# An attention block on one core: p transposed as pairs of bf16, the engines' orders rearranged, and V loaded in two pieces

## The chip, the cores and the metric

The kernel runs on one core of a Trainium2 chip. Its time is the device time of one execution in microseconds (us); "before" is the median of three runs. One further execution was recorded by the profiler, and all durations below come from that one.

## What is computed

The reference projects x to queries for 32 heads of width 192, attends over a cache of 512 keys and values, and projects the result back:

```python
B, Sq, D = 8, 112, 640
H, Sk, Dh = 32, 512, 192
q = (x @ wq).reshape(B, Sq, H, Dh).transpose(0, 2, 1, 3)
scores = einsum("bhqd,bhkd->bhqk", q, k_cache) * Dh ** -0.5
p = softmax(scores, axis=-1)
o = einsum("bhqk,bhkd->bhqd", p, v_cache)
out = o.transpose(0, 2, 1, 3).reshape(B, Sq, H * Dh) @ wo
```

All inputs and the output are bf16. The two caches are 50 MB each and are read once.

## The kernel before

The work is cut into 64 groups. A group is four heads of one batch element (two pairs of heads, `pr` 0 and 1). `groups` lists them by head group (eight heads) and batch element. Every operation is entered into a `Plan` as one block on one engine, with the tokens that it reads and writes; the order in which blocks are entered is the order in which an engine runs them, and `Plan.solve` turns tokens into semaphore waits. A token with fewer slots than versions makes a writer wait for the readers of the version that it overwrites.

A loop over `g` (lines 540 to 606) enters one iteration of a software pipeline. In an iteration TensorE (PE) works on four groups at once:

- scores of group g: `s_mains` (L302, L304, contraction 128) for heads 2, 3, 0, 1, then `s_tails` (L317, L319, contraction 64, two at a time in the two halves of the array), into PSUM banks 0 to 3;
- `pv_tails` of g-2 (L404), the last 64 columns of p times V, two heads side by side;
- `pt` of g-1 (L367), the transposes of the normalised p, four blocks of 112x128 for each head, into bank PTB; pair 0 before the output projection and pair 1 between the two `q_stage` blocks;
- `o_stage` of g-2 (L432 and, for the last 128 output columns, L446), the output projection;
- `q_stage` of g+2 (L261), the queries, into banks 0 and 1;
- `pv_mains` of g-1 (L389).

VectorE (DVE) takes the scores out of PSUM with the row minimum of the negated scores (`smax`, L331), copies transposed p (`evac_pt`, L377), inverts the row sums (L350), normalises p (`norm`, L357) and, at the end of its iteration, adds the output projection to an accumulator (`oacc`, L468/L469). ScalarE (ACT) copies the results of PV (`evac_m` L413, `evac_t` L419), computes the four exponentials (L341) and copies the queries (`evac_q`, L271) after the second and after the fourth exponential. GpSimd (POOL) makes a copy of the queries with the partition halves swapped (L282, L284). For the last head group, `o_final` (L480) transposes the sums back and `evac_final` (L488) copies them out.

All loads are issued by one queue, SP's, in a fixed order: for two groups at a time K, K, V, V (L220, L229) and then at most one piece of wq or wo (L237, L245) for the next head group; these pieces end with group 51. K is loaded by a transposing DMA, 768 KB for a group; V by one plain DMA of 128 rows, each with four runs of 1,536 bytes. There are six buffers for K and six for V. The key order inside a row of 512 scores is that of K's transposed layout; `QJ` says which quarter of V belongs to which quarter of p.

Of the kernel before, what the change touches and what calls it, by code (L numbers as in the profile page):

```python
# [142 lines left out]
def build_mha_kernel(nc, x, k_cache, v_cache, wq, wo, out):  # L143
# [12 lines left out]
    QJ = [0, 2, 1, 3]  # L156
# [18 lines left out]
    with ExitStack() as es:  # L175
# [17 lines left out]
        ident = sb("ident", [128, 128], BF16)  # L193
        nmx = sb("nmx", [SQ, 8], F32)
# [4 lines left out]
        psb = ps[:].bitcast(BF16)  # L199

# [23 lines left out]
        def load_v(g):  # L224
            u, hg, b, half = group(g)
            h0 = hg * HG + 4 * half

            def fn(e):
                return e.dma_start(vt[g % NVB][:, :, :], v_cache[b, h0:h0 + 4].rearrange("u (r q) d -> r u (q d)", q=4))  # L229
            P.add("SP", f"v{g}", fn, writes=[("vt", g)], dma=True)  # L230
# [63 lines left out]
        def s_mains(g, h):  # L294
            em, _, om, _ = q_tiles(g, h)
            pr, cols = h // 2, slice(256 * (h % 2), 256 * (h % 2) + 256)
            n = 2 * g + pr
            k = kt[g % NKB]
            cs = slice(h * 128, (h + 1) * 128)

            def fn(e):
                e.matmul(ps[0:SQ, 2 * pr, cols], em, k[:, :, 0, cs], start=(h % 2 == 0), stop=False,  # L302
                         skip_group_check=True)
                return e.matmul(ps[0:SQ, 2 * pr + 1, cols], om, k[:, :, 2, cs], start=(h % 2 == 0), stop=False,  # L304
                                skip_group_check=True)
            P.add("PE", f"S{g}.{h}", fn, reads=[("kt", g), ("qs", n), ("w", n)],
                  writes=[(f"bank{2 * pr + i}", 2 * g) for i in range(2)])

        def s_tails(g, pr):
            k = kt[g % NKB]  # L310

            def fn(e):
                for h in (2 * pr, 2 * pr + 1):
                    _, lo, _, hi = q_tiles(g, h)
                    cols = slice(256 * (h % 2), 256 * (h % 2) + 256)
                    cs = slice(h * 128, (h + 1) * 128)
                    e.matmul(ps[0:SQ, 2 * pr, cols], lo, k[0:64, :, 1, cs], start=False, stop=True,  # L317
                             skip_group_check=True)
                    mm = e.matmul(ps[0:SQ, 2 * pr + 1, cols], hi, k[64:128, :, 1, cs], start=False, stop=True,  # L319
                                  skip_group_check=True)  # L320
                return mm
            n = 2 * g + pr
            P.add("PE", f"St{g}.{pr}", fn, reads=[("kt", g), ("qs", n), ("w", n)],
                  writes=[(f"bank{2 * pr + i}", 2 * g) for i in range(2)])

        def smax(g, h):
            n = 4 * g + h
            pr, cols = h // 2, slice(256 * (h % 2), 256 * (h % 2) + 256)

            def fn(e):  # L330
                return e.tensor_scalar(s_sb[:, n % 4, :].rearrange("p (a c) -> p a c", a=2),  # L331
                                       ps[0:SQ, 2 * pr:2 * pr + 2, cols], -scale, None, op0=ALU.mult, op1=ALU.min,
                                       accum_out=nmx[:, n % 8:n % 8 + 1])
            P.add("DVE", f"mx{g}.{h}", fn, reads=[(f"bank{2 * pr + i}", 2 * g) for i in range(2)],
                  writes=[("s", n), ("nmx", n)])
# [17 lines left out]
        def norm(g, h):  # L353
            n = 4 * g + h

            def fn(e):
                return e.tensor_scalar(pn_sb[:, n % 8, :], p_sb[:, n % 4, :], rinv[:, n % 8:n % 8 + 1], None,  # L357
                                       op0=ALU.mult)
            P.add("DVE", f"nm{g}.{h}", fn, reads=[("p", n), ("rinv", n // 2)], writes=[("pn", n)])

        def pt(g, pr):
            def fn(e):
                for h in range(2):
                    n = 4 * g + 2 * pr + h
                    for j in range(4):
                        c = (4 * h + j) * SQ
                        mm = e.transpose(psb[:, PTB, c:c + SQ], pn_sb[:, n % 8, j * 128:(j + 1) * 128],  # L367
                                         ident[0:SQ, 0:SQ])
                return mm
            P.add("PE", f"PT{g}.{pr}", fn, reads=[("pn", 4 * g + 2 * pr), ("pn", 4 * g + 2 * pr + 1), ("ident", 0)],  # L370
                  writes=[("ptb", 2 * g + pr)])

        def evac_pt(g, pr):
# [4 lines left out]
            P.add("DVE", f"ep{g}.{pr}", fn, reads=[("ptb", n)], writes=[("pT", n)])  # L378

        def pv_mains(g, pr):  # L380
# [3 lines left out]
            def fn(e):  # L384
                for h in range(2):
                    u = 2 * pr + h
                    for j in range(4):
                        d0 = QJ[j] * 192 + 64 * h
                        mm = e.matmul(ps[:, MB, (2 * pr + h) * SQ:(2 * pr + h + 1) * SQ], v[:, u, d0:d0 + 128],  # L389
                                      pT[:, n % 3, (4 * h + j) * SQ:(4 * h + j + 1) * SQ],  # L390
                                      start=(j == 0), stop=(j == 3))
# [3 lines left out]
        def pv_tails(g):  # L395
            v = vt[g % NVB]

            def fn(e):
                for pr in range(2):
                    n = 2 * g + pr  # L400
                    for j in range(4):
                        for h in range(2):
                            d0 = QJ[j] * 192 + (128 if h == 0 else 0)
                            mm = e.matmul(ps[64 * h:64 * h + 64, TB, pr * SQ:(pr + 1) * SQ],  # L404
                                          v[:, 2 * pr + h, d0:d0 + 64],
                                          pT[:, n % 3, (4 * h + j) * SQ:(4 * h + j + 1) * SQ],
                                          start=(j == 0), stop=(j == 3))
# [15 lines left out]
        def o_stage(g):  # L423
# [13 lines left out]
            P.add("PE", f"O{g}", fn, reads=[("oT", g)] + wos, writes=[("ob", 2 * u)])  # L437
# [17 lines left out]
        def oacc(g):  # L455
# [15 lines left out]
            for part, name, tok in ((1, "acc5", ("tb", 2 * g + 1)), (0, "acc4", ("ob", 2 * u))):  # L471
# [3 lines left out]
        def o_final(g):  # L475
            u, hg, b = groups[g][:3]

            def fn(e):
                for c in range(DC):
                    mm = e.transpose(psb[0:SQ, OB, c * 128:(c + 1) * 128], oTf[:, b % 2, c, :], ident[:, :])  # L480
                return mm
            P.add("PE", f"OF{b}", fn, reads=[("oTf", b), ("ident", 0)], writes=[("ob", 2 * u + 1)])

        def evac_final(g):
            u, hg, b = groups[g][:3]

            def fn(e):
                return e.activation(o_out[b], psb[0:SQ, OB, 0:D], ACTF.Copy)  # L488
            P.add("ACT", f"ef{b}", fn, reads=[("ob", 2 * u + 1)], writes=[("oo", b)])
# [6 lines left out]
        def init_pool():  # L496
# [4 lines left out]
                  reads=[("id0", 0)], writes=[("ident", 0)])  # L501

# [37 lines left out]
        for g in range(-2, NG + 3):  # L540
            qver = 2 * g + 1

            if ok(g):
                for h in (2, 3, 0, 1):
                    s_mains(g, h)
                s_tails(g, 0)
                s_tails(g, 1)
            fin = ok(g - 3) and groups[g - 3][1] == NHG - 1 and groups[g - 3][5]
            if fin:
                o_final(g - 3)  # L550
            if ok(g - 2):
                pv_tails(g - 2)
# [10 lines left out]
            if ok(g - 1):  # L563
                pv_mains(g - 1, 0)
                pv_mains(g - 1, 1)

            if ok(g - 2):
                evac_m(g - 2)
            if fin:
                evac_final(g - 3)  # L570
            if ok(g - 2):
                evac_t(g - 2)
            if ok(g):
                exp(g, 0)
                exp(g, 1)
            if ok(g + 2):
                evac_q(g + 2, 0, qver)
            if ok(g):
                exp(g, 2)
                exp(g, 3)  # L580
            if ok(g + 2):
                evac_q(g + 2, 1, qver)

# [5 lines left out]
            if ok(g):  # L589
                smax(g, 2)  # L590
                smax(g, 3)
            if ok(g - 1):
# [8 lines left out]
            if ok(g - 2) and groups[g - 2][5]:  # L601
                oacc(g - 2)
# [80 lines left out]
```

## Time and profile before

| | |
|---|---|
| median of three runs | 501.61 us (496.06 to 502.46) |
| profiled execution: device time | 505.89 us |
| profiled execution: span, first to last instruction | 503.9 us |
| mean granted TensorE clock | 0.986 |
| busy: PE / DVE / ACT / POOL | 452.3 / 361.7 / 288.1 / 86.5 us |
| moved by DMA | 119.88 MB, mean 238 GB/s |
| V loads, K loads | 64 each; median from issue to landing 6.6 and 8.5 us |

A line of a group view reads: line, engine, operation, output from input, count, then busy time and mean duration of one. A PE duration holds the pipeline's depth too, so the pace of a row of matmuls is read from the start times in the timeline, not from the duration of one. "PEld" is the loading of the stationary operand. "SPq" in a chain or a timeline is the SP queue while it issues a DMA: an issue lasts longer when the descriptors find no room.

### The profile page before, as it was taken

Reading aid. Unit: us, or ns where it says so; the run is one execution under the profiler, and the core shown is the slowest. Engines: PE = TensorE matmul, PEld = TensorE weight load, DVE = VectorE, ACT = ScalarE, POOL = GpSimd, SP = SyncE. Lnnn points to the kernel's source line nnn. Section 1 sums busy time; section 2 is a strip of 40 time slices with the busy share of each in tenths; the row PEclk is TensorE's granted clock in tenths of the full one; section 3 lists DMA queues with packets and bytes.
Section 4 is the critical chain, followed back from the end, with each engine's and each line's share of the span. In section 5 each row is a group of like instructions: output and inputs, shape, how many; then the busy total and the mean of one; then the engine's idle time right before and its main releaser. Section 6 shows DMA issues by size and latency. Waiting matters only on the chain.

```text
span 503.9 us, 18575 instructions
## 1 busy us (share of the span) xinstructions
PE 452.3 (90%) x7976; PEld 403.8 (80%) x7976; DVE 361.7 (72%) x1105; ACT 288.1 (57%) x778; POOL 86.5 (17%) x262
## 2 busy tenths in 40 slices
PE   4749898989998988998997999999999899999985
PEld 4639787878987977887987888898888788888974
DVE  0728867787888777767776788787777777787781
ACT  2616645556656545655654566565566567666762
POOL 1202212112112212212211112211121121112100
PEclk9989989999999999999999999999999999999999
DMA  8999999999999999999999999999999999999910
GB/s 188 227 267 263 255 301 273 221 223 256 258 278 249 236 228 230 238 260 265 231 200 252 270 264 245 276 264 231 233 262 246 272 228 258 245 257 230 269 44 23
DMA packets 255026, 119.88 MB, mean 238 GB/s; under 512 B 204896, under 2 KB 254944, under 8 KB 254944
## 3 DMA queue, kind: packets, MB, share of 16 engines
q1 hardware_dynamic: 254944, 118.70, 106.3%
q8 instruction: 62, 1.02, 0.9%
q14 instruction: 20, 0.16, 0.1%
HBM read 66.06 MB, written 1.15 MB: 133 GB/s over the span
## 4 chain that ended last, share of the span: by engine, by line
DMA 35%; PE 30%; SPq 25%; ACT 4%; DVE 3%; issue 2%; POOL 0%; DVEq 0%
DMA kt<-in_k_cache_dram 32%; SPq L220 20%; PE ps L432 6%; PE ps L261 5%; PE ps L367 3%; PE ps L302 3%; ACT p_sb L341 3%; PE ps L404 2%; PE ps L304 2%; PE ps L317 2%; SPq L229 2%; PE ps L389 2%; DMA wo_sb<-in_wo_dram 2%; PE ps L446 1%; SPq L245 1%
## 5 line engine op out<-in xcount | busy, mean ns | idle before, releaser
L331 DVE TENSOR_SCALAR_CACHE_REDUCE s_sb<-ps 112x512 f32<-112x512 f32 x256 | 165.5, 683 | 50.2 <-PE ps L319 50.2
L341 ACT ACTIVATE p_sb<-s_sb,nmx 112x512 bf16<-112x512 f32 x256 | 181.2, 712 | 3.7 <-DVE s_sb L331 3.7
L261 PE MATMUL ps<-xT,wq_sb 128*128 128x112 bf16 x1920 | 118.6, 216 | 16.0 <-DMA wq_sb<-in_wq_dram 7.3
L377 DVE COPY pT<-ps 128x896 bf16<-128x896 bf16 x128 | 79.8, 623 | 69.9 <-PE ps L367 69.9
L261 PEld LDWEIGHTS ps<-xT,wq_sb 128*128 128x128 bf16 x1920 | 104.0, 100 | 16.6 <-DMA wq_sb<-in_wq_dram 7.3
L282 POOL COPY wt<-qs 64x168 int32<-64x168 int32 x128 | 44.4, 347 | 383.9 <-ACT qs L271 383.9
L271 ACT ACTIVATE qs<-ps 128x336 bf16<-128x336 f32 x128 | 56.6, 442 | 84.7 <-PE ps L261 84.6
L432 PE MATMUL ps<-oT,wo_sb 128*128 128x112 bf16 x1536 | 86.6, 213 | 3.4 <-DMA wo_sb<-in_wo_dram 1.9
L357 DVE TENSOR_SCALAR pn_sb<-p_sb,rinv 112x512 bf16<-112x512 bf16 x256 | 83.3, 368 | 4.5
L432 PEld LDWEIGHTS ps<-oT,wo_sb 128*128 128x128 bf16 x1536 | 76.6, 98 | 10.8 <-ACT p_sb L341 3.1
L419 ACT ACTIVATE oT<-ps 128x224 bf16<-128x224 f32 x64 | 22.8, 356 | 105.9 <-PE ps L404 105.9
L367 PE MATMUL ps<-ident,pn_sb 112*128 112x112 bf16 x1024 | 72.7, 214 | 0.0
L389 PE MATMUL ps<-pT,vt 128*128 128x112 bf16 x1024 | 61.5, 213 | 1.0 <-DVE pT L377 1.0
L302 PE MATMUL ps<-kt,qs 128*112 128x256 bf16 x128 | 38.0, 297 | 25.1 <-DMA kt<-in_k_cache_dram 20.1
L367 PEld LDWEIGHTS ps<-ident,pn_sb 112*128 112x128 bf16 x1024 | 55.2, 98 | 5.2 <-issue 0.2
L389 PEld LDWEIGHTS ps<-pT,vt 128*128 128x128 bf16 x1024 | 53.7, 98 | 1.5 <-DVE pT L377 1.4
L341 ACT ACTIVATION_READ_ACCUMULATOR p_sb<-s_sb,nmx 112x1 f32 x256 | 48.8, 190 | 0.0
L302 PEld LDWEIGHTS ps<-kt,qs 128*112 128x112 bf16 x128 | 16.5, 129 | 35.2 <-DMA kt<-in_k_cache_dram 13.3
L284 POOL COPY wt<-qs 64x168 int32<-64x168 int32 x128 | 41.4, 323 | 7.9
L404 PE MATMUL ps<-pT,vt 128*64 128x112 bf16 x1024 | 37.9, 217 | 0.0
L404 PEld LDWEIGHTS ps<-pT,vt 128*64 128x64 bf16 x1024 | 28.3, 111 | 10.9 <-issue 10.1
L413 ACT ACTIVATE oT<-ps 128x448 bf16<-128x448 f32 x64 | 34.4, 537 | 4.6 <-PE ps L389 4.6
(33 smaller groups left out, 489.3 us busy)
## 6 DMA issues: line engine op xcount, KB each, us to landing
vt<-in_v_cache_dram SPq DMA_DIRECT2D x64, 768.0 KB, 6.6
wq_sb<-in_wq_dram SPq DMA_DIRECT2D x16, 480.0 KB, 9.0
wo_sb<-in_wo_dram SPq DMA_DIRECT2D x16, 480.0 KB, 8.4
out_dram<-accT SPq DMA_DIRECT2D x8, 140.0 KB, 7.1
kt<-in_k_cache_dram SPq DMA_TRANSPOSE x64, 8.5
xT<-in_x_dram SPq DMA_TRANSPOSE x3, 4.3
```

The lines of the kernel that those rows point to most:

```text
L220: return e.dma_start_transpose(kt[g % NKB][:].rearrange("p a m c -> p (a m) c"), k_cache[b, h0:h0 + 4].rearrange("u (r q) d -> (u r) (q d) ...
L261: mm = e.matmul(ps[:, pr, c * SQ:(c + 1) * SQ], wq_sb[:, hg % 2, dc, c0 + 128 * c:c0 + 128 * (c + 1)], xT[:, dc, b * SQ:(b + 1) * SQ], sta ...
L271: return e.activation(qs[:, n % 6, :, :], ps[:, pr, 0:3 * SQ].rearrange("p (c s) -> p c s", c=3), ACTF.Copy)
L302: e.matmul(ps[0:SQ, 2 * pr, cols], em, k[:, :, 0, cs], start=(h % 2 == 0), stop=False, skip_group_check=True)
L331: return e.tensor_scalar(s_sb[:, n % 4, :].rearrange("p (a c) -> p a c", a=2), ps[0:SQ, 2 * pr:2 * pr + 2, cols], -scale, None, op0=ALU.mu ...
L341: return e.activation(p_sb[:, n % 4, :], s_sb[:, n % 4, :], ACTF.Exp, bias=nmx[:, n % 8:n % 8 + 1], scale=-1.0, accum_out=rsum[:, n % 8:n ...
L357: return e.tensor_scalar(pn_sb[:, n % 8, :], p_sb[:, n % 4, :], rinv[:, n % 8:n % 8 + 1], None, op0=ALU.mult)
L367: mm = e.transpose(psb[:, PTB, c:c + SQ], pn_sb[:, n % 8, j * 128:(j + 1) * 128], ident[0:SQ, 0:SQ])
L377: return e.tensor_copy(pT[:, n % 3, :], psb[:, PTB, 0:8 * SQ])
L389: mm = e.matmul(ps[:, MB, (2 * pr + h) * SQ:(2 * pr + h + 1) * SQ], v[:, u, d0:d0 + 128], pT[:, n % 3, (4 * h + j) * SQ:(4 * h + j + 1) * SQ],
L404: mm = e.matmul(ps[64 * h:64 * h + 64, TB, pr * SQ:(pr + 1) * SQ], v[:, 2 * pr + h, d0:d0 + 64], pT[:, n % 3, (4 * h + j) * SQ:(4 * h + j ...
L432: mm = e.matmul(ps[:, OB, dcc * SQ:(dcc + 1) * SQ], wo_sb[:, wb, 3 * (2 * half + pr) + c, dcc * 128:(dcc + 1) * 128], oT[:, g % 3, pr, c, ...
```

## The change

It has four parts. V of a group is loaded by two DMAs, rows 0 to 119 and rows 120 to 127, on the same semaphore. p is transposed as words: `smax` writes the scores of two key quarters interleaved, so that two neighbouring bf16 of the normalised p form one 4-byte word; `pt` transposes the 512 bf16 of a head as 256 words in two blocks of 112x128 f32 against an f32 identity, and PV reads its moving operand with a step of two elements (`p_block`); `norm` raises p to at least 2^-126, so that no word is subnormal. The order on PE becomes: tails of the scores before their mains, `pv_tails` of g-1 at the end of the iteration, after `pv_mains`, and `o_final` just before it. On ACT the four exponentials come in a row and both `evac_q` after them; on DVE `oacc` comes before the second `evac_pt`.

```diff
@@ -153,7 +153,7 @@
     scale = float(DH) ** -0.5
-    QJ = [0, 2, 1, 3]
+    TINY = 2.0 ** -126
     NKB, NVB = 6, 6
@@ -191,6 +191,7 @@
         ident = sb("ident", [128, 128], BF16)
+        identf = sb("identf", [SQ, SQ], F32)
         nmx = sb("nmx", [SQ, 8], F32)
@@ -198,6 +199,9 @@
         psb = ps[:].bitcast(BF16)
+        pnw = pn_sb[:].rearrange("p n k -> p (n k)").bitcast(F32)
         o_out = [accT[0:SQ, b, :, :].rearrange("p c s -> p (c s)").bitcast(BF16)[:, 0:D] for b in range(B)]
@@ -225,9 +229,12 @@
             h0 = hg * HG + 4 * half
-            def fn(e):
-                return e.dma_start(vt[g % NVB][:, :, :], v_cache[b, h0:h0 + 4].rearrange("u (r q) d -> r u (q d)", q=4))
-            P.add("SP", f"v{g}", fn, writes=[("vt", g)], dma=True)
+            def fn(r0, r1):
+                src = v_cache[b, h0:h0 + 4].rearrange("u (r q) d -> r u (q d)", q=4)
+                return lambda e: e.dma_start(vt[g % NVB][r0:r1, :, :], src[r0:r1])
+            for r0, r1 in ((0, 120), (120, 128)):
+                P.add("SP", f"v{g}.{r0}", fn(r0, r1), writes=[("vt", g)], dma=True)
         def load_wq(hg, lp, after=()):
@@ -299,9 +306,9 @@
             def fn(e):
-                e.matmul(ps[0:SQ, 2 * pr, cols], em, k[:, :, 0, cs], start=(h % 2 == 0), stop=False,
+                e.matmul(ps[0:SQ, 2 * pr, cols], em, k[:, :, 0, cs], start=False, stop=True,
                          skip_group_check=True)
-                return e.matmul(ps[0:SQ, 2 * pr + 1, cols], om, k[:, :, 2, cs], start=(h % 2 == 0), stop=False,
+                return e.matmul(ps[0:SQ, 2 * pr + 1, cols], om, k[:, :, 2, cs], start=False, stop=True,
                                 skip_group_check=True)
@@ -314,9 +321,9 @@
                     cs = slice(h * 128, (h + 1) * 128)
-                    e.matmul(ps[0:SQ, 2 * pr, cols], lo, k[0:64, :, 1, cs], start=False, stop=True,
+                    e.matmul(ps[0:SQ, 2 * pr, cols], lo, k[0:64, :, 1, cs], start=(h % 2 == 0), stop=False,
                              skip_group_check=True)
-                    mm = e.matmul(ps[0:SQ, 2 * pr + 1, cols], hi, k[64:128, :, 1, cs], start=False, stop=True,
+                    mm = e.matmul(ps[0:SQ, 2 * pr + 1, cols], hi, k[64:128, :, 1, cs], start=(h % 2 == 0), stop=False,
                                   skip_group_check=True)
@@ -328,7 +335,7 @@
             def fn(e):
-                return e.tensor_scalar(s_sb[:, n % 4, :].rearrange("p (a c) -> p a c", a=2),
+                return e.tensor_scalar(s_sb[:, n % 4, :].rearrange("p (c a) -> p a c", a=2),
                                        ps[0:SQ, 2 * pr:2 * pr + 2, cols], -scale, None, op0=ALU.mult, op1=ALU.min,
@@ -354,28 +361,32 @@
             def fn(e):
-                return e.tensor_scalar(pn_sb[:, n % 8, :], p_sb[:, n % 4, :], rinv[:, n % 8:n % 8 + 1], None,
-                                       op0=ALU.mult)
+                return e.tensor_scalar(pn_sb[:, n % 8, :], p_sb[:, n % 4, :], rinv[:, n % 8:n % 8 + 1], TINY,
+                                       op0=ALU.mult, op1=ALU.max)
             P.add("DVE", f"nm{g}.{h}", fn, reads=[("p", n), ("rinv", n // 2)], writes=[("pn", n)])
...
                     n = 4 * g + 2 * pr + h
-                    for j in range(4):
-                        c = (4 * h + j) * SQ
-                        mm = e.transpose(psb[:, PTB, c:c + SQ], pn_sb[:, n % 8, j * 128:(j + 1) * 128],
-                                         ident[0:SQ, 0:SQ])
-                return mm
-            P.add("PE", f"PT{g}.{pr}", fn, reads=[("pn", 4 * g + 2 * pr), ("pn", 4 * g + 2 * pr + 1), ("ident", 0)],
-                  writes=[("ptb", 2 * g + pr)])
+                    for t in range(2):
+                        c = (2 * h + t) * SQ
+                        w0 = (n % 8) * (SK // 2) + t * 128
+                        mm = e.transpose(ps[:, PTB, c:c + SQ], pnw[:, w0:w0 + 128], identf[:, :])
+                return mm
+            P.add("PE", f"PT{g}.{pr}", fn, reads=[("pn", 4 * g + 2 * pr), ("pn", 4 * g + 2 * pr + 1), ("identf", 0)],
+                  writes=[("ptb", 4 * g + pr)])
         def evac_pt(g, pr):
...
                 return e.tensor_copy(pT[:, n % 3, :], psb[:, PTB, 0:8 * SQ])
-            P.add("DVE", f"ep{g}.{pr}", fn, reads=[("ptb", n)], writes=[("pT", n)])
+            P.add("DVE", f"ep{g}.{pr}", fn, reads=[("ptb", 4 * g + pr)], writes=[("pT", n)])
+        def p_block(n, h, q):
+            return pT[:, n % 3, :].rearrange("p (h t s a) -> p h t a s", h=2, t=2, a=2)[:, h, q // 2, q % 2, :]
         def pv_mains(g, pr):
@@ -385,10 +396,9 @@
                     for j in range(4):
-                        d0 = QJ[j] * 192 + 64 * h
+                        d0 = j * 192 + 64 * h
                         mm = e.matmul(ps[:, MB, (2 * pr + h) * SQ:(2 * pr + h + 1) * SQ], v[:, u, d0:d0 + 128],
-                                      pT[:, n % 3, (4 * h + j) * SQ:(4 * h + j + 1) * SQ],
-                                      start=(j == 0), stop=(j == 3))
+                                      p_block(n, h, j), start=(j == 0), stop=(j == 3))
                 return mm
@@ -400,11 +410,10 @@
                         for h in range(2):
-                            d0 = QJ[j] * 192 + (128 if h == 0 else 0)
+                            d0 = j * 192 + (128 if h == 0 else 0)
                             mm = e.matmul(ps[64 * h:64 * h + 64, TB, pr * SQ:(pr + 1) * SQ],
                                           v[:, 2 * pr + h, d0:d0 + 64],
-                                          pT[:, n % 3, (4 * h + j) * SQ:(4 * h + j + 1) * SQ],
-                                          start=(j == 0), stop=(j == 3))
+                                          p_block(n, h, j), start=(j == 0), stop=(j == 3))
                 return mm
@@ -434,7 +443,7 @@
                 return mm
-            P.add("PE", f"O{g}", fn, reads=[("oT", g)] + wos, writes=[("ob", 2 * u)])
+            P.add("PE", f"O{g}", fn, reads=[("oT", g)] + wos, writes=[("ob", u)])
             if not last:
@@ -468,7 +477,7 @@
                 return go
-            for part, name, tok in ((1, "acc5", ("tb", 2 * g + 1)), (0, "acc4", ("ob", 2 * u))):
+            for part, name, tok in ((1, "acc5", ("tb", 2 * g + 1)), (0, "acc4", ("ob", u))):
                 P.add("DVE", f"oa{part}.{u}", fn(part), reads=[tok] + ([] if copy else [(name, ver - B)]),
@@ -477,16 +486,17 @@
                 for c in range(DC):
-                    mm = e.transpose(psb[0:SQ, OB, c * 128:(c + 1) * 128], oTf[:, b % 2, c, :], ident[:, :])
-                return mm
-            P.add("PE", f"OF{b}", fn, reads=[("oTf", b), ("ident", 0)], writes=[("ob", 2 * u + 1)])
+                    mm = e.transpose(psb[0:SQ, PTB, c * 128:(c + 1) * 128], oTf[:, b % 2, c, :], ident[:, :])
+                return mm
+            P.add("PE", f"OF{b}", fn, reads=[("oTf", b), ("ident", 0)],
+                  writes=[("ptb", 4 * (g + 1) + 2)])
         def evac_final(g):
...
             def fn(e):
-                return e.activation(o_out[b], psb[0:SQ, OB, 0:D], ACTF.Copy)
-            P.add("ACT", f"ef{b}", fn, reads=[("ob", 2 * u + 1)], writes=[("oo", b)])
+                return e.activation(o_out[b], psb[0:SQ, PTB, 0:D], ACTF.Copy)
+            P.add("ACT", f"ef{b}", fn, reads=[("ptb", 4 * (g + 1) + 2)], writes=[("oo", b)])
         def store(b):
@@ -499,6 +509,8 @@
                   reads=[("id0", 0)], writes=[("ident", 0)])
+            P.add("POOL", "id2", lambda e: e.tensor_copy(identf[:], ident[0:SQ, 0:SQ]), reads=[("ident", 0)],
+                  writes=[("identf", 0)])
         GH = B * GPU
@@ -541,15 +553,11 @@
             if ok(g):
-                for h in (2, 3, 0, 1):
+                s_tails(g, 1)
+                s_tails(g, 0)
+                for h in range(4):
                     s_mains(g, h)
-                s_tails(g, 0)
-                s_tails(g, 1)
-            fin = ok(g - 3) and groups[g - 3][1] == NHG - 1 and groups[g - 3][5]
-            if fin:
-                o_final(g - 3)
-            if ok(g - 2):
-                pv_tails(g - 2)
+            fin = ok(g - 2) and groups[g - 2][1] == NHG - 1 and groups[g - 2][5]
             if ok(g - 1):
@@ -563,23 +571,22 @@
                 pv_mains(g - 1, 1)
+            if fin:
+                o_final(g - 2)
+            if ok(g - 1):
+                pv_tails(g - 1)
             if ok(g - 2):
                 evac_m(g - 2)
-            if fin:
-                evac_final(g - 3)
-            if ok(g - 2):
                 evac_t(g - 2)
             if ok(g):
-                exp(g, 0)
-                exp(g, 1)
+                for h in range(4):
+                    exp(g, h)
             if ok(g + 2):
                 evac_q(g + 2, 0, qver)
-            if ok(g):
-                exp(g, 2)
-                exp(g, 3)
-            if ok(g + 2):
                 evac_q(g + 2, 1, qver)
+            if fin:
+                evac_final(g - 2)
             if ok(g):
@@ -589,6 +596,8 @@
                 smax(g, 3)
+            if ok(g - 2) and groups[g - 2][5]:
+                oacc(g - 2)
             if ok(g - 1):
@@ -598,8 +607,6 @@
                 norm(g, 3)
-            if ok(g - 2) and groups[g - 2][5]:
-                oacc(g - 2)
             if ok(g + 2):
```

## The prediction

> **What bounds the kernel now.** I read the page first, then the windows, the SP queue's timeline, PE's timeline and last the DMA packet records.
>
> ```profile
> PE 452.3 (90%) x7976; PEld 403.8 (80%) x7976; DVE 361.7 (72%) x1105; ACT 288.1 (57%) x778; POOL 86.5 (17%) x262
> DMA  8999999999999999999999999999999999999910
> ...
> q1 hardware_dynamic: 254944, 118.70, 106.3%
> q8 instruction: 62, 1.02, 0.9%
> ```
>
> Two resources look full: PE at 90%, the DMA engines at 9 tenths or more nearly everywhere. An average does not say which sets the pace, so I cut the span.
>
> ```profile
> 200.00:300.00 100.00, 92.57 (x1644) 82.43 (x1643) 73.52 (x225) 57.54 (x158) 17.43 (x52) 0.98 1.14 247
> 402.00:474.00 72.00, 71.49 (x1275) 63.40 (x1272) 55.00 (x169) 46.20 (x124) 13.41 (x40) 1.00 1.13 242
> ```
>
> From 402 us, when wq and wo are all loaded, PE is busy for 71.49 of 72 us: PE sets the pace there. In the chain its output projections of every second group start at 401.55 and 473.30, five pairs of groups apart: 14.35 us a pair. From 200 to 300 PE idles 7%, and SP's queue shows why.
>
> ```profile
> 261.56 1.08 SPq L229 DMA_DIRECT2D vt<-in_v_cache_dram  x2
> 262.69 0.50 SPq L245 DMA_DIRECT2D wo_sb<-in_wo_dram  x1
> 263.24 12.91 SPq L220 DMA_TRANSPOSE kt<-in_k_cache_dram  x2
> 276.25 1.08 SPq L229 DMA_DIRECT2D vt<-in_v_cache_dram  x2
> ```
>
> SP waits for no buffer here; two K issues take 12.91 us where one can take 3.56 (its minimum): the rings are full, so DMA sets the pace. The packet records (start, duration and size of each packet, counted in steps of 0.1 us) show one period: K flows for 2.2 us at full rate, a gap of 1.9, K again for 2.2, then a gap of 7.2 to 9.7 with the two V and the wo or wq. First K flows begin at 59.6 and 402.2 us, 23 pairs apart: 14.9 us a pair. In the gaps most K packets stand still until the last DMA engine arrives: K moves only when all sixteen are there. What makes one late is the 16 KB packet of the queue "q8 instruction", 1.05 us at the median; PE's 15,952 matmuls and weight loads come in 62 of them. One lands just after each first K (gap 1.9; the one time without, at 430.7, 0.8), and one among the V packets: gaps of 8.5 on average in 17 pairs from 125 us, 7.3 in the two (278.6 and 321.8 us) without one or with it at the very start. So an instruction packet among V costs 1.2 us a pair. The records do not name the engine.
>
> **The change part by part.** *V in two pieces.* A V packet takes 65 ns. Before, 512 packets over sixteen engines are 32 each. 120 rows are 15 x 8, so I take fifteen engines with 32 packets and one with none, and the 8 rows one each on eight of these: 36 there. The price is 4 x 65 ns x 2 loads = 0.52 us a pair on those eight; the gain is 1.2 us a pair if the idle engine is the one that fetches PE's instructions, as it then has 4.2 us (64 x 65 ns) to spare. It stays +0.52 if the fetch is on one of the eight, and about 0 if on one of the other seven. Ends from rows: -1.2 (no imbalance felt) to +4.2 a pair (every V packet twice as long, because eight neighbouring rows may share a way into memory). I take -1.2 + 0.52. No row decides between these; that the engine left without V is the late one is the guess on which the forecast stands, made because the gaps show one engine late and never several, and its failure is the first rival. Over 23 pairs, 21 with such a fetch: -25 + 12 = -13 us.
>
> [...]
>
> The second V issue costs SP 0.5 us (a V issue's median is 522 ns), 1.0 us a pair. It hides in the K issues, which stand 12.91 us against 2 x 3.56; without that cover, 64 x 0.5 = 32 us. Behind it wait wo or wq and the next K, whose data could not flow yet.
>
> *Transposes.*
>
> ```profile
> L367 PE MATMUL ps<-ident,pn_sb 112*128 112x112 bf16 x1024 | 72.7, 214 | 0.0
> L367 PEld LDWEIGHTS ps<-ident,pn_sb 112*128 112x128 bf16 x1024 | 55.2, 98 | 5.2 <-issue 0.2
> L302 PEld LDWEIGHTS ps<-kt,qs 128*112 128x112 bf16 x128 | 16.5, 129 | 35.2 <-DMA kt<-in_k_cache_dram 13.3
> ...
> 447.09 0.56 PE L367 MATMUL ps<-ident,pn_sb 112*128 112x112 bf16 x8
> 447.48 0.90 PE L261 MATMUL ps<-xT,wq_sb 128*128 128x112 bf16 x15
> ```
>
> Eight transposes take 0.39 us (447.09 to 447.48), 49 ns each; sixteen a group become eight. No row has an f32 operand. [...] I take 49, the nearest row by shape.
>
> [...]
>
> *Orders.* In PE's timeline the projection starts when `evac_t` ends (444.05 to 444.57 for eight transposes, 0.52 instead of 0.39): 0.1 us. Mains into banks 0 and 1 wait for `evac_q`: 0.1 us. With `pv_tails` a half iteration earlier and two tails ahead, both go: 0.18 us. ACT's exponentials in a row end before the second query block; `evac_q` 1 ends near 6.2 us of the iteration, before the next tails of banks 0 and 1. `oacc` (0.8 us) fills DVE's 1.19 us wait ahead of the second `evac_pt`; where it doesn't fit, `pv_mains` waits some 0.3 us every second group, and `pv_tails` behind it. `o_final` waits for DVE as before.
>
> *Nothing I price elsewhere.* PV's step of two (ends 0 and twice its pace: +1.3 us a group), the interleaved score write and the second operation in `norm` (ends 0, and to the pace of L331, +0.3 us each, which DVE's 17 of 72 idle us nearly hold): 0.
>
> **The sum.** Where PE sets the pace, 0.39 + 0.18 = 0.57 us a group over 12 groups (402 to 484): -7 us. Elsewhere PE's gain hides behind DMA: PE would need 14.35 - 1.14 = 13.2 us a pair, DMA 14.9 - 0.6 = 14.3. V: -13 us. 1,024 fewer PE instructions are four instruction packets, half of them between K: -2 us. Together -22: 505.89 becomes 484; the median is 0.99 of the profiled execution's time, so 480.
>
> **The rivals.** *The idle engine isn't the fetching one.* For: the records name no engine, and fifteen others could be it. Against: nothing in this case's rows. V then costs 0 to +12 us; with -9 for the rest, 497 to 509 on the profile's scale, 492 to 504 on the median's: within 2%.
>
> *V packets get slower.* With fifteen engines each taking neighbouring rows, two may write through one place. For: a twentieth of V's packets take 96 ns or more, against 65. Against: wo's packets keep 55 ns at the median. At 96, an engine's 72 packets a pair take 6.9 us instead of 4.2: +2.7, less the 1.2 hidden fetch, +1.5 a pair over 23 pairs = +35, and PE's part saves little: about 530. From about 85 ns on the kernel is slower by over 2%.
>
> [...]
>
> **How the numbers follow.** Forecast 0.52, idle engine elsewhere 0.22, slow V packets 0.14, slow words or PV 0.12. The predicted time is 480, its own range 470 to 491. To leave out no more than two in ten the range reaches over the second case and the start of the third: 468 to 522. A difference of 2% (10 us) is about what a measurement of this kernel can tell from none. Faster 0.52; within 2% 0.22; slower 0.26.
>
> **What would show it.** Right: gaps with V near 7.8 us, PE idle in 200 to 300 down to or below 5%, 8 transposes in 0.39 us or less a group, no wait of L419 on L404, periods after 402 near 13.2. Wrong: V packets above 80 ns, transposes at 100 ns or more, first K flows 15 us apart or more, or PE waiting for `evac_pt` in every group.

## The result and the profile after

The changed kernel takes 592.97 us (median of 4 runs, 592.39 to 595.44) against 501.30 us before (496.06 to 502.46): ratio 1.1867, 95% interval 1.1789 to 1.1945. It was predicted 4% faster and is 19% slower. Here and below medians are over all runs, while a ratio and its interval leave out the runs in which a kernel was slower as a whole. The profiled execution took 592.47 us, with a span of 590.7.

From the page: engines, DMA and the two main queues.

```profile
span 590.7 us, 17607 instructions
...
PE 471.7 (80%) x7464; PEld 440.6 (75%) x7464; DVE 365.0 (62%) x1105; ACT 305.6 (52%) x778; POOL 85.8 (15%) x263
...
DMA  8999999999999999999999999999999999999992
...
q1 hardware_dynamic: 255392, 118.70, 111.1%
q8 instruction: 58, 0.95, 0.7%
```

PE's share of the span falls from 90% to 80%, and DMA is now at 9 tenths up to the slice before the last; before it was down to 1 and 0 in the last two slices. The bytes are the same (118.70 MB), and the q1 packets fill 111.1% of a span that is 17% longer: each byte costs more DMA time. The chain that ended last gives SP's queue 43% and DMA 36% of the span, PE 15%.

The same windows as before, the second one again after the last weights have landed (us, busy time of PE, PEld, DVE, ACT and POOL, granted clock, DMA share, GB/s):

```profile
200.00:300.00 100.00, 87.35 (x1382) 81.86 (x1380) 64.89 (x198) 53.42 (x136) 15.90 (x48) 0.92 1.14 213
484.00:560.00 76.00, 72.07 (x1207) 68.23 (x1205) 54.83 (x167) 47.57 (x120) 13.23 (x40) 0.96 1.16 203
```

From 200 to 300, 247 GB/s have become 213, and the granted clock 0.98 has become 0.92; PE ran 1,382 matmuls where it ran 1,644 (the words alone take 6% of all matmuls away, 7,464 for 7,976; e1 below, which has the words and not the split, runs 1,561 in this window). Its busy time hides part of the loss, as a matmul takes 63 ns on average against 59 in e1 (87.35 us over 1,382, 91.84 over 1,561). In the second window PE no longer sets the pace as it did before (71.49 of 72): it idles 4 of 76 us at a clock of 0.96.

The waits (engine, line, what it waited for: us in total, times, longest us), after the change, then one line of e1 below, which has everything but the split, and one of the kernel before:

```profile
PE ps L324 <- DMA kt<-in_k_cache_dram: 72.9, 25, 5.6
...
PEld ps L324 <- DMA kt<-in_k_cache_dram: 42.6, 15, 5.7
...
ACT oT L428 <- PE ps L414: 2.8, 3, 1.3
```

```profile
PE ps L324 <- DMA kt<-in_k_cache_dram: 24.9, 19, 4.2
```

```profile
ACT oT L419 <- PE ps L404: 105.9, 56, 5.7
```

PE waits 72.9 us for K; in e1 24.9. ACT's wait for the tails, 105.9 us before, is 2.8.

SP's queue:

```profile
254.90 1.79 SPq L235 DMA_DIRECT2D vt<-in_v_cache_dram  x4
256.73 0.63 SPq L244 DMA_DIRECT2D wq_sb<-in_wq_dram  x1
257.41 14.71 SPq L224 DMA_TRANSPOSE kt<-in_k_cache_dram  x2
272.17 1.95 SPq L235 DMA_DIRECT2D vt<-in_v_cache_dram  x4
```

Four V issues in 1.8 to 1.95 us instead of two in 1.08: 0.7 to 0.9 us more, where 1.0 was priced. But two K issues stand 14.71 us instead of 12.91: the queue drains more slowly.

What drains more slowly is in the packet records (counted as in the prediction; the sum is over all packets, divided by sixteen engines):

```
                          before            after
V packets, 1,536 B        65 / 77 ns        120 / 121.7 ns    median / mean
  sum over 16 engines     157.6 us          249.3 us
wq packets, 768 B         mean 39 ns        mean 53.8 ns
wo packets, 1,280 B       mean 59 ns        mean 87.0 ns
K packets, 256 B
  sum over 16 engines     325.0 us          330.8 us
```

The typical V packet takes almost twice as long. The weights' packets, issued by the same queue, become longer too; K's hardly do. First K flows go from 69.6 to 483.5 us, 23 pairs: 18.0 us a pair where it was 14.9. That splits the loss of the profiled execution without a rest: 10.0 us before the first of these pairs, 71.3 in the 23 pairs, 5.5 behind them, together the 86.8 between the spans of 503.9 and 590.7.

### The profile page after: what moved, and what is told of

It reads as the page before. It is cut to its first block, busy times and chain, and to the rows that moved or that the text cites. A ratio compares the mean times of both kernels' runs of the same rounds, so it can differ in the third digit from the quotient of the medians.

```text
span 590.7 us, 17607 instructions
## 1 busy us (share of the span) xinstructions
PE 471.7 (80%) x7464; PEld 440.6 (75%) x7464; DVE 365.0 (62%) x1105; ACT 305.6 (52%) x778; POOL 85.8 (15%) x263
## 2 busy tenths in 40 slices
DMA packets 255470, 119.82 MB, mean 203 GB/s; under 512 B 205344, under 2 KB 255392, under 8 KB 255392
## 3 DMA queue, kind: packets, MB, share of 16 engines
q1 hardware_dynamic: 255392, 118.70, 111.1%
## 4 chain that ended last, share of the span: by engine, by line
SPq 43%; DMA 36%; PE 15%; issue 2%; DVE 2%; ACT 1%; DVEq 0%
DMA kt<-in_k_cache_dram 36%; SPq L224 33%; SPq L235 6%; PE ps L441 3%; PE ps L324 3%; PE ps L268 2%; PE ps L309 2%; PE ps L375 1%; PE ps L400 1%; PE ps L311 1%; SPq L252 1%; SPq L244 1%; DVE s_sb L338 1%; SPq L211 1%; PE ps L414 1%
## 5 line engine op out<-in xcount | busy, mean ns | idle before, releaser
L268 PEld LDWEIGHTS ps<-xT,wq_sb 128*128 128x128 bf16 x1920 | 108.3, 101 | 17.1 <-issue 7.8
L441 PE MATMUL ps<-oT,wo_sb 128*128 128x112 bf16 x1536 | 95.1, 224 | 16.0 <-DMA wo_sb<-in_wo_dram 10.8
L441 PEld LDWEIGHTS ps<-oT,wo_sb 128*128 128x128 bf16 x1536 | 90.3, 104 | 17.4 <-ACT p_sb L348 11.4
L324 PE MATMUL ps<-kt,qs 64*112 64x256 bf16 x128 | 37.6, 314 | 74.1 <-DMA kt<-in_k_cache_dram 72.9
L384 DVE COPY pT<-ps 128x896 bf16<-128x896 bf16 x128 | 79.6, 622 | 27.0 <-PE ps L375 25.8
L364 DVE TENSOR_SCALAR pn_sb<-p_sb,rinv 112x512 bf16<-112x512 bf16 x256 | 91.1, 397 | 4.5
L278 ACT ACTIVATE qs<-ps 128x336 bf16<-128x336 f32 x128 | 53.7, 438 | 50.0 <-PE ps L268 48.0
L324 PEld LDWEIGHTS ps<-kt,qs 64*112 64x112 bf16 x128 | 17.3, 135 | 81.8 <-DMA kt<-in_k_cache_dram 42.6
L375 PE MATMUL ps<-identf,pn_sb 112*128 112x112 f32 x512 | 76.0, 274 | 0.4 <-ACT accT L498 0.4
L375 PEld LDWEIGHTS ps<-identf,pn_sb 112*128 112x128 f32 x512 | 58.7, 150 | 2.2 <-DVE accT L478 1.7
L309 PE MATMUL ps<-kt,qs 128*112 128x256 bf16 x128 | 41.5, 325 | 0.0
L311 PE MATMUL ps<-kt,qs 128*112 128x256 bf16 x128 | 39.1, 306 | 0.0
```

Of the source, the lines that this page charges most:

```text
L268: mm = e.matmul(ps[:, pr, c * SQ:(c + 1) * SQ], wq_sb[:, hg % 2, dc, c0 + 128 * c:c0 + 128 * (c + 1)], xT[:, dc, b * SQ:(b + 1) * SQ], sta ...
L278: return e.activation(qs[:, n % 6, :, :], ps[:, pr, 0:3 * SQ].rearrange("p (c s) -> p c s", c=3), ACTF.Copy)
L309: e.matmul(ps[0:SQ, 2 * pr, cols], em, k[:, :, 0, cs], start=False, stop=True, skip_group_check=True)
L375: mm = e.transpose(ps[:, PTB, c:c + SQ], pnw[:, w0:w0 + 128], identf[:, :])
L384: return e.tensor_copy(pT[:, n % 3, :], psb[:, PTB, 0:8 * SQ])
L441: mm = e.matmul(ps[:, OB, dcc * SQ:(dcc + 1) * SQ], wo_sb[:, wb, 3 * (2 * half + pr) + c, dcc * 128:(dcc + 1) * 128], oT[:, g % 3, pr, c, ...
```

## The experiments

Three theories were set against each other first: V's packets are slow because two engines write through one **place** at a time; because the load goes over fifteen **engines**, not sixteen; because there are **two DMAs** where one was.

**e1: the changed kernel with V in one load.**

```
-            for r0, r1 in ((0, 120), (120, 128)):
+            for r0, r1 in ((0, 128),):
```

> The changed kernel with V in one DMA of 128 rows again; p as words and the orders stay. All three theories of the slow V packets (120 ns at the median after the change, 65 before) expect 65 ns here. Place theory (packets are slow because an engine's eight neighbouring rows share a way into memory with those of another engine), engine theory (fifteen engines instead of sixteen), two-DMA theory (the second DMA itself): the 87 us of the change all come from V, so this runs at or a little below the kernel before, 480 to 500 us. If p as words or the orders cost part of the 87 us, it lands above 505 us.

496.75 us (491.20 to 498.23) against 503.94 in this group of runs: 0.9855 (0.9735 to 0.9975). V's packets are back at 65 ns, mean 77.6. Words and orders together gain about 7 us (1 to 13 by the interval); the whole loss is V's.

**e2: the kernel before with the split alone** (the V hunk of the change).

> The kernel before with nothing changed but V in two DMAs, rows 0 to 119 and 120 to 127. If V alone makes the loss: V packets at 120 ns, 16 to 18 us a pair of groups instead of 14.9, 575 to 605 us. If the loss needs the other parts of the change, below 540 us.

602.47 us in one run: 1.20 of before. V's packets take 120 ns at the median, mean 122.4. The split alone makes the loss, without the words and the orders.

**e3: two loads, but of all 128 rows and two heads each.**

```
-            for r0, r1 in ((0, 120), (120, 128)):
+            for u0, u1 in ((0, 2), (2, 4)):
...
-                return lambda e: e.dma_start(vt[g % NVB][r0:r1, :, :], src[r0:r1])
+                return lambda e: e.dma_start(vt[g % NVB][:, u0:u1, :], src[:, u0:u1])
```

> The changed kernel with V in two DMAs cut by heads: 128 rows each, two of the four runs of a row. Place and engine theory: rows and engines lie as in one DMA, so V packets stay at 65 ns and the time is that of the kernel with one V DMA within 1% (480 to 500 us). Two-DMA theory: the second DMA costs what it does in the changed kernel, 570 to 600 us.

497.44 us (492.32 to 501.35): 0.9878 (0.9828 to 0.9927), as e1. Its issues (KB each, median us to landing):

```profile
vt<-in_v_cache_dram SPq DMA_DIRECT2D x128, 384.0 KB, 5.2
```

Twice as many V issues, packets at 65 ns, mean 77.9: the second DMA costs nothing that shows, neither in SP's queue nor in the packets' times. The theory of two DMAs is out.

**e4: 112 and 16 rows.**

```
-            for r0, r1 in ((0, 120), (120, 128)):
+            for r0, r1 in ((0, 112), (112, 128)):
```

> The changed kernel with V cut at row 112: 112 rows are seven for each of sixteen engines, 16 rows one for each. Engine theory: sixteen engines again, 65 ns, 480 to 500 us. Place theory: seven neighbouring rows of one engine and those of others still meet, but not all the time, so V packets of the large piece lie between 65 and 120 ns and those of the 16 rows, which lie side by side in 16 partitions, at 200 ns or more; 510 to 570 us. Two-DMA theory: about 590 us.

554.01 us in one run; V's packets at 93 ns, mean 103.8. Among the packets under 512 B (204,896 before) are small semaphore writes of 4 B, and e3 has 1,024 more of them (205,920): its second load of 128 rows adds 16 for each of 64 loads, as many as there are engines. So the count is read here as one write from each engine that shares a load, an inference, as no record names an engine. The changed kernel has 448 more than before (205,344), 7 for each of 64 loads, that is 15 + 8 = 23 instead of 16 for 120 and 8 rows; here it is 1,024 more, 16 for each, so 16 + 16 = 32. By this count both parts use all sixteen engines, and the packets are still slow. The theory of fifteen engines can't explain that.

**e5: loads by themselves.** The kernel issues V loads of one shape at a time and waits for each before the next.

> No attention at all: only loads of V rows, each awaited before the next, eight of each shape, and the output is zeros. Shapes: 128 rows; 120 rows from partition 0; 112 rows from 0; 64 rows from 0; the same 64 rows into partitions 32 to 95; 60 rows into 32 to 91; 8 rows into 120 to 127. [...] Engine theory (fewer than sixteen engines are slow): 60 from 32 as slow as 120, both loads of 64 rows at 65. A theory of the source (neighbouring rows of the cache read at once): both loads of 64 rows alike, whatever they cost.

```profile
r<-in_v_cache_dram SPq DMA_DIRECT2D x8, 768.0 KB, 4.4
r64at<-in_v_cache_dram SPq DMA_DIRECT2D x16, 384.0 KB, 3.9
r<-in_v_cache_dram SPq DMA_DIRECT2D x8, 720.0 KB, 5.8
```

128 rows land in 4.4 us, 120 rows, fewer bytes, in 5.8, with packets of 65 and 114 ns. So no K, no weights and no second part are needed. 60 rows, which by the count of small writes go over fifteen engines (e5's 944, e6's 1,778 and e11's 3,308 come out with 15 for each load of 60 rows), kept 65 ns when they began at partition 32: that is the second strike against the engine theory. But the place theory missed too: by the author's estimate it made 120 ns for 64 rows from partition 0, 75 to 95 for 112 rows and over 200 for the 8 rows, and all three showed 65 at the median. A load this short leaves each engine few packets (16 with 64 rows over sixteen engines, 4 with 8 rows over eight), and the longer way from first to last (2.2 us from partition 0, 1.8 from 32) hinted that the packets' own times don't show the queueing. It needed more loads in flight.

**e10: the same shapes, eight loads queued at a time.**

```
+                    for i in range(8):
+                        e.dma_start(t[p0:p0 + rows, i, :, :], f(8 * rep + i)[0:rows]).then_inc(dt, 16)
+                    n += 128
+                    e.wait_ge(dt, n)
```

> Loads only, zeros as output, as in the run with awaited loads, but eight loads of a shape are queued before any is awaited, so that nothing an engine holds back hides a slow write. Shapes: 128, 120, 120 with source rows four times as far apart, 112, 96, 64 from partition 0, the same 64 from 32, 60 from 32, 8 from 120. Place theory with a way into memory of about 26 GB/s (two engines at 118 ns a packet): 65, 118, 118, 75 to 90, 80 to 95, 118, 65, 65, and 230 for the 8 rows, where four engines share a way. Source theory: the wide 120 rows differ from the plain 120, and both loads of 64 rows are alike. Engine theory, already weak: 60 rows as slow as 120.

```
rows, from partition      median packet    GB/s        (three bursts of eight loads each)
128 from 0                68 ns            348 to 358
120 from 0                118 to 121       202 to 213
120 from 0, other source  407 to 422       214 to 233  (packets of 6,144 B)
112 from 0                84 to 106        237 to 299
 96 from 0                107 to 112       228 to 238
 64 from 0                128 to 129       196 to 203
 64 from 32               65               263 to 281
 60 from 32               65               300 to 316
  8 from 120              225 to 239       60 to 64
```

The same 64 rows, from the same source, take 129 ns a packet when they are written to partitions 0 to 63 and 65 when to 32 to 95. Nothing differs but the place they are written to. Other source rows don't help 120 rows. So the place decides; this much of the place theory is now shown. The rest is a picture that the numbers fit, though no record shows which engines share a way: one engine alone moves 23.6 GB/s (1,536 B in 65 ns); two on one way need 118 to 129 ns each, together 24 to 26 GB/s; four need 225 to 239, together 26 to 27. The way's rate is known only roughly, as part of the packets of the 8 rows still take 65 ns, and over a whole burst these rows move 60 to 64 GB/s, more than two such ways would carry. Two of the theory's numbers were off: 112 rows were slower than the 75 to 90 ns expected in one burst of three (106; the others 84 and 85), 96 rows slower than 80 to 95 in all. And why 128 rows show no sharing, as if each engine had a way for itself, isn't in the records, which name no engine: that the rows of a 120-row load are dealt as eight neighbours to an engine stays an inference.

**e6 and e11: which engine fetches PE's instructions?** The forecast's gain stood on the guess that it is the one a 120-row load leaves out. Thousands of matmuls run beside awaited loads of 64, 60, 56, 52, 44 and 40 rows from partition 32, which by the count of small writes (16, 15, 14, 13, 11 and 10 a load) leave out 0, 1, 2, 3, 5 and 6 of the sixteen engines.

> No attention: TensorE runs 8,000 matmuls without a wait, so that its instruction packets keep coming, beside thirty loads each of 64, 60, 56 and 40 rows from partition 32 on, each awaited; the output is zeros. 64 rows divide over sixteen engines, 60 over fifteen, 56 over fourteen, 40 over ten. If TensorE's instructions come over the engine that a 120-row load leaves out, loads of 64 rows that meet an instruction packet land up to 1 us later and those of 60 rows never do. If they come over another engine, loads of 60 rows are delayed as well, and 56 or 40 tell whether it is among the first fourteen or ten.

e6 (400.89 us) had few overlaps. The two 64-row loads that lay under an instruction packet for at least 0.8 us landed late (2.31 and 2.78 us; the slowest without one 2.03), so did the one such 60-row load (2.92; the slowest without one 2.31), and none of the four such 40-row loads (1.71 to 1.78). The fetching engine is among those that 60 rows use and not among those that 40 rows use: one overlap was too thin to stand on.

> As the first run with TensorE's instruction packets beside loads, with sixty loads each of 60, 56, 52 and 44 rows (fifteen, fourteen, thirteen and eleven engines); the output is zeros. In that run no load on ten engines was late and one on fifteen was, by 1 us. If the instruction packets come over the engine that a 120-row load leaves out, no load here is late where it meets one; if over another of the last six, loads of 60 rows that overlap a packet by most of its 1.05 us land 0.7 to 1 us later, and the shape from which this stops names the engine.

e11 (792.83 us) gave more, and a better count than the landing times: how many 16 KB packets **start** inside a load, more than 0.1 us before its last packet ends. A load takes 1.85 of each 3.15 us, so about 16 or 17 of 29 would, if packets took no notice of loads. With 60 rows 2 of 29 did, with 56 rows 0 of 29, with 52 rows 0 of 29, with 44 rows 10 of 28. So here an instruction packet waits until its engine has done its queued load packets; its engine works on the 52-row load, over thirteen engines, and not on the 44-row load, over eleven. If smaller loads use the first of the larger ones' engines, which no record shows, it is the twelfth or thirteenth of them. Whatever the order, a load over fifteen engines uses it.

**e7 and e8: words and orders apart.** e7 is the kernel before with the words (transposes, interleaved scores, `TINY`, the V blocks in order), e8 the kernel before with the new orders and bank tokens. V is one load in both.

> The kernel before with p transposed as words alone; engine orders and the single V load as before. A word transpose takes 98 ns in the changed kernel's trace (four in 0.39 us) against 49 for a bf16 one, so PE gains nothing by the words, only 1,024 instructions and four instruction packets fewer. If the 1.4% of the words and orders together come from the orders: within 1% of before, 497 to 506 us. If they come from the words: 490 to 497.

e7: 502.89 us (499.66 to 505.25) against 505.84: 0.9984 (0.9937 to 1.0031). The words bring nothing. The reason is in PE's timeline and in the groups (line, shapes, count | busy us, mean ns | idle before), here of the changed kernel:

```profile
505.49 0.55 PE L375 MATMUL ps<-identf,pn_sb 112*128 112x112 f32 x4
505.88 1.30 PE L441 MATMUL ps<-oT,wo_sb 128*128 128x112 bf16 x23
```

```profile
L375 PE MATMUL ps<-identf,pn_sb 112*128 112x112 f32 x512 | 76.0, 274 | 0.4 <-ACT accT L498 0.4
L375 PEld LDWEIGHTS ps<-identf,pn_sb 112*128 112x128 f32 x512 | 58.7, 150 | 2.2 <-DVE accT L478 1.7
```

Four word transposes take 0.39 us from the first to what follows (505.49 to 505.88): 98 ns each, where bf16 took 49. Half as many at twice the price. Their weight load takes 150 ns against 98.

> The kernel before with the other engine orders alone; p is transposed as before and V is one load. If the gain of words and orders together is that of the orders: 490 to 498 us. If it is that of the words: 500 to 506 us.

e8: 498.91 us (497.00 to 499.75): 0.9893 (0.9813 to 0.9972), a gain of about 5 us by the ratio (1.4 to 9.4 by its interval) that the orders bring. Which of the orders brings it, no run separates.

**e9 and e12: K of two groups in one transposing load.** As the prediction reads the packet records, each start of K waits for all sixteen engines (gaps of 0.8 us, and of 1.9 with an instruction packet). If that start has a price of its own, one load of 1,536 KB for a pair must beat two; the edit is on e1, from the second head group (group 16) on, where K is entered for every second group:

```
-        kt = [sb(f"kt{j}", [128, 2, 3, 512], BF16) for j in range(NKB)]
+        kp = [sb(f"kt{j}", [128, 2, 3, 1024], BF16) for j in range(NKB // 2)]
+        kt = [kp[j // 2][:, :, :, 512 * (j % 2):512 * (j % 2) + 512] for j in range(NKB)]
...
+                if g >= GH:
+                    return e.dma_start_transpose(kp[g % NKB // 2][:].rearrange("p a m c -> p (a m) c"),
+                                                 k_cache[b, h0:h0 + 8].rearrange("u (r q) d -> (u r) (q d)", q=4))
...
```

> The changed kernel with V in one DMA again and, from group 16 on, K of two groups in one transposing DMA of 1,536 KB instead of two. Each K load starts with a stop until the last DMA engine has arrived (gap of 1.9 us between the two K of a pair with an instruction packet in it, 0.8 without). If the stop belongs to the start of a load, 24 pairs lose 0.8 to 1.9 us each: DMA's period goes from 14.7 to about 13.3 us, PE's 13.7 us takes over, and the kernel takes 470 to 482 us. If the stop belongs to the amount of K, or the instruction packet merely moves to the gap with V, it stays within 1% of the kernel with two K loads (491 to 501 us).

484.43 us (483.13 to 486.23) against 504.95: 0.9627 (0.9563 to 0.9691): a little above the 470 to 482 us expected, and faster than both kernels. The same window, first of e1, then of e9:

```profile
200.00:300.00 100.00, 91.84 (x1561) 86.32 (x1559) 74.72 (x228) 62.31 (x160) 18.35 (x56) 0.98 1.14 247
```

```profile
200.00:300.00 100.00, 95.90 (x1660) 90.27 (x1657) 79.25 (x241) 66.06 (x170) 19.27 (x59) 1.00 1.19 266
```

DMA moves 266 instead of 247 GB/s, and PE gets 1,660 instead of 1,561 matmuls through. In the packet records a pair takes 13.8 us (118.1 to 297.6, 13 pairs) where e1 takes 14.6 over the same 13 pairs (118.2 to 308.3). The 0.8 us saved are as much as the gap between two K without an instruction packet, so the price of a start fits. The stops by instruction packets stay: of the first 14 pairs loaded in this way after 130 us, K stands for 1.3 to 1.4 us inside the single load in the 11 where an instruction packet started about 0.5 us earlier, and for 0.7, 0 and 0 us in the three without one. PE is then nearly the bound: 92% busy, as the page has it, and it still waits 15.4 us for K.

```profile
PE 442.1 (92%) x7464; PEld 415.7 (86%) x7464; DVE 363.9 (76%) x1105; ACT 303.5 (63%) x778; POOL 84.6 (18%) x263
```

> The kernel with the other orders alone (p transposed as before, V in one load) and K of two groups in one transposing DMA from group 16 on. The words were worth 0.2% alone, so that this should come within 1% of the version with words, 482 to 492 us; if fewer instruction packets matter once PE sets the pace, the words are worth more and it lands at 490 us or above.

e12, the orders and K in pairs without the words: 485.62 us (483.63 to 487.04), 0.9608 (0.9556 to 0.9659). It can't be told from e9: the words bring nothing here either, where PE is busier than before.

## Why the prediction was wrong

**V's packets: the step that failed.** Of the ends -1.2 and +4.2 us a pair the prediction took -1.2 + 0.52, with the packets' price unchanged. The upper end, every V packet twice as long, is nearly what happened: 120 ns for 65, and +3.1 us a pair. The term was -13 us; the runs make it about +96 (592.97 for the changed kernel, 496.75 for e1; the two came from different groups of runs, whose medians before are 501.30 and 503.94). The rival "V packets get slower" had the place and the sign, but chose 96 ns, from the slowest twentieth of the packets before, and so 530 us. Two things were missing from it: 120 instead of 96, and the weights' packets, which it left at their price and which grew by a third to a half (39 to 53.8 ns and 59 to 87.0). Over the sixteen engines V costs 249.3 - 157.6 = 91.7 us more, the weights 34.4 - 25.1 and 38.3 - 25.8, 21.8 together; of these 113 us some 96 are felt in the time. The evidence against the rival, that wo's packets kept 55 ns beside V, was evidence about V in 128 rows only.

**The fetching engine.** "The engine left without V is the late one" was a guess, and e11 refutes it: the fetching engine works on loads of 60, 56 and 52 rows too, so it isn't the one that a load over fifteen engines leaves out. If loads take the engines in order, which no record shows, it is the twelfth or thirteenth, one of the seven for which the prediction itself had about 0 instead of -13 us. The picture behind the guess holds in part. In e11, where each load is awaited, an instruction packet mostly waits for its engine's queued load packets instead of pushing them aside (2 of 87 started inside a load of 60, 56 or 52 rows). In the kernel, where DMA is at 9 tenths nearly throughout, it does hold up K, as e9's stops inside one load show; what it does among V's packets no run separates.

**The imbalance** of 0.52 us a pair can't be seen beside the rest. e3's two loads without a split by rows show that the second issue on SP is hidden, as priced.

**Words.** 49 ns was the nearest row by shape; 98 was measured. So 0.39 us a group became 0, as in e7 (0.9984). The case of slow words, with its part in the 0.12, did not come either: at 98 ns for half as many the words cost nothing that shows, and no run shows a price above that. 58 instruction packets instead of 62 came as counted, and their 2 us can't be told from nothing in e7.

**Orders.** Right in direction, too small in size. ACT's wait for the tails (105.9 us) is gone, and e8 gains about 5 us (1.4 to 9.4), where 0.18 us a group over 12 groups made 2. Where in the kernel it is gained stays open: over the 23 pairs K comes 14.7 us apart in e8 and 14.9 before, but 14.7 to 14.8 in e7 too, which gains nothing. With the words e1 gains 7; the prediction had 7 for the orders and words where PE sets the pace and 2 for the packets. That these agree is luck: words at nothing instead of 5, orders at 5 instead of 2.

**What was priced at nothing.** It was right that these cost nothing to speak of. PV with a step of two keeps its pace nearly (sixteen matmuls in a row took 0.95 us before and 0.98 after), and the interleaved scores do too (683 and 687 ns). `norm` went from 368 to 397 ns, but not by its second operation: e7, which has that operation and the old orders, shows 368, and e8, with the new orders and without it, 398. So it is the orders that lengthen it, hidden on DVE; why, no run shows. In the changed kernel (the rows before were 213 and 368 ns), then in e7 and in e8:

```profile
L400 PE MATMUL ps<-pT,vt 128*128 128x112 bf16 x1024 | 63.7, 213 | 3.9 <-DVE pT L384 2.1 <-issue 1.9
...
L364 DVE TENSOR_SCALAR pn_sb<-p_sb,rinv 112x512 bf16<-112x512 bf16 x256 | 91.1, 397 | 4.5
```

```profile
L364 DVE TENSOR_SCALAR pn_sb<-p_sb,rinv 112x512 bf16<-112x512 bf16 x256 | 83.3, 368 | 4.5
```

```profile
L357 DVE TENSOR_SCALAR pn_sb<-p_sb,rinv 112x512 bf16<-112x512 bf16 x256 | 91.4, 398 | 4.5
```

**The signs it named.** Two signs of "wrong" appeared, V packets above 80 ns and K flows more than 15 us apart, and a third to within 2 ns (transposes at 98, where 100 was named). The fourth, PE waiting for `evac_pt` in every group, did not: 3 waits, 2.1 us.

## What to carry to other kernels

A DMA's rows are more than bytes: how many partitions, and from which one, decides what a packet costs (65 to 239 ns for 1,536 B in e10), by the picture above because engines share a way into the memory. So a transfer that is whole at 128 rows should not be cut by partitions without measuring its packets; cut it along the free axis instead (e3), which cost nothing that shows. Where an unknown cost has an end that wipes out the gain several times over, the forecast must not stand on the other end because of a guess about which engine is late. And where each transposing load begins with a stop (in e9 half as many saved 0.8 us a pair), try fewer and larger ones: here that was worth 12 us (484.43 against 496.75), more than the words and orders together (7).

## What the runs showed of the hardware

With eight loads queued a 1,536 B packet takes 65 to 68 ns, 118 to 129 or 225 to 239, as if one, two or four engines wrote through one way. The partition a tile begins at alone moves 64 rows from 200 to 270 GB/s. One transposing load of 1,536 KB instead of two saves 0.8 us a pair (14.6 to 13.8). A 16 KB instruction packet seldom starts while its engine has load packets queued (2 of 87 started inside the awaited loads of 52 to 60 rows). A transpose of f32 words takes 98 ns where one of bf16 with the same columns takes 49. And PE's clock fell with the slower loads: with waits of up to 5.6 us for K the granted clock over the profiled execution was 0.917, against 0.983 in e1, which differs by the split alone, and 0.986 before.
